# Operand places, piece look-ahead and one job's start in a Fourier-plus-MLP kernel

## The chip, the cores and the metric

The kernel runs on one core of one Trainium2 chip. The metric is device time in microseconds for one execution; lower is better. A core has TensorE (PE, matmuls; PEld its weight loads), VectorE (DVE), ScalarE (ACT), GpSimd (POOL, which here mainly issues DMAs) and SyncE (SP, which only issues DMAs). They run beside each other and wait for each other by semaphores. SBUF is the on-chip memory of 128 partitions, PSUM holds the results of matmuls in eight banks.

## What is computed

x has 2048 rows (tokens) and 640 columns. It is normalized, and three terms are added: x itself, the real part of a two-dimensional Fourier transform, and an MLP that mixes tokens. All is float32.

```python
x = A_x
xn = _layernorm(x, axis=-1)
# A: Fourier mixing
a = einsum("bsd,ed->bse", xn, dft_hid_re)
b = einsum("bsd,ed->bse", xn, dft_hid_im)
A = einsum("ts,bse->bte", dft_seq_re, a) - einsum("ts,bse->bte", dft_seq_im, b)
# B: token MLP, on layernorm(xn) again
u = gelu(einsum("bsd,sf->bdf", _layernorm(xn), w1) + b1)      # F = 1728
B = (einsum("bdf,fs->bds", u, w2) + b2).transpose(0, 2, 1)
return x + A + B
```

## The kernel before

**Pieces.** Every product of two float32 operands is made of three matmuls: each operand is cut into a high part (ACT copies it to float32r, line 131) and a low part (DVE subtracts, line 134); then come high x high, high x low and low x high (`three`, lines 139 to 144). An operand that is used once is a *piece*: `cut_piece` (161) gives its `top` (the ACT copy) and its `bottom` (the DVE subtraction). The pieces lie in three tiles of 5,120 bytes a partition (tags cut0 to cut2), taken in turn. An operand that is used often is cut once and kept.

**Steps and turns.** The work on PE is a list of `steps`, each with the top and the bottom of its piece and its matmuls. `turn_of(i)` (921) writes turn i into the queues: the loads due then, the reads (PSUM copies and adds), the row stages' sums, the top of the piece of step i + AHEAD (AHEAD is 2), the extras (in the column passes the sums of raw pieces), timed work, one or more *jobs* from a list, the bottom of that same piece, more jobs, and last the matmuls of step i. This order is written out by hand; each engine works its queue off in order.

**Stages.** They follow each other on PE:
- *First columns* (`first_columns`, 422): 18 steps, 240 matmuls of 512 columns, for the first block of the sequence transform, while x arrives and is normalized. The order of the first turns is the string START (45); from step 8 on the turns run in the loop at 946. At turn 10 five PSUM copies are due (`reads[10]`, 456, the copies themselves on line 448), at 16 and 18 five more.
- *Column passes* (`columns`, 493), seven of 32 steps and 216 matmuls of 512 columns: the stationary operand is a part of the kept rows (tile n, four slabs of 16,384 bytes), the moving one a piece of the transform's matrix. The first three passes use rows 0 to 1023, in slabs 0 to 3, the last four rows 1024 to 2047, in slabs 4 to 7. In each pass, seven products take the place of eight (Strassen's scheme), so raw pieces are added and subtracted in place (DVE, line 137), two sums at a time, at fixed steps of the pass; the raw pieces come in by DMA from SP, sixteen for each pass, with names B11 to B22 for their quarter. The steps' stationary operand changes slab from step to step: (i, q) uses slab q, or 4 + q in the last four passes.
- *Row stages* (`row_steps`, 697): hid (8 x 7 steps), up0 and up1 (7 x 7 each), down0 and down1 (8 x 7 each), with matmuls of 320 columns. Here the piece is the stationary operand (640, 512 or 384 columns) and the kept tiles shid, sup and sdown, in the same slabs, are the moving one.

**Jobs.** What prepares kept operands is cut into jobs and handed to later turns. The first sums (24 jobs for slabs 0 to 3: `sums_of_rows`, 272) enter the list at turn 9 (867); the rows of slabs 4 to 7 (42 jobs) at turn 18 (875). Up to turn 17 a turn takes two jobs, one ahead of the bottom and one behind it; from 18 on the tables at 56 tell.

**Places.** A tile gets its place in SBUF when its tag is first declared, one behind the other, each rounded up to 32 bytes. In order, with bytes a partition: b1_sb (56), b2_sb (64), slab4 and slab5 (17,920 each), `one` (4), slab7 (17,920), mv, norm and again (128 each), slabs 0 to 3 (17,920 each), the two tiles of raw pieces (16,384 and 17,920), two of 6,144, the three for pieces, v (5,120), slab6 (17,920), and the small working tiles.

Of the kernel before, what the change touches and what calls it, by code (L numbers as in the profile page):

```python
# [8 lines left out]
F32 = mybir.dt.float32  # L9
R32 = mybir.dt.float32r  # L10
# [4 lines left out]
P = 128  # L15
S = 2048
D = 640
F = 1728
NS = S // P
ND = D // P  # L20
# [5 lines left out]
CH = 512  # L26
NC = S // CH
H2 = D // 2
EPS = 1e-5
AHEAD = 2  # L30
LOADS = 4
WARM = 13

BLOCK = 18
# [33 lines left out]
def fnet_plus_mixer(  # L68
# [36 lines left out]

    b1_sb = keep.tile([P, NFB], F32, name="b1_sb")
    b2_sb = keep.tile([P, NS], F32, name="b2_sb")
    out_rows = [out[t * P : (t + 1) * P, :] for t in range(NS)]
    x_rows = [x[t * P : (t + 1) * P, :] for t in range(NS)]

# [7 lines left out]
    y_part = [[dram.tile([P, ND, CH], F32, name=f"y{m}{c}") for c in range(NC)] for m in range(2)]  # L118


    one = keep.tile([P, 1], F32, name="one")
    nc.vector.memset(one, 1.0)
    nc.scalar.activation(one, one, AF.Sqrt)
    idle = keep.tile([P, CH], BF16, name="idle", tag="slab7")
# [31 lines left out]
    loads, sums, reads, extras, timed = (defaultdict(list) for _ in range(5))  # L156
    jobs = []

    cut_turn = [0]

    def cut_piece(source, n):

        held = {}

        def top():
            cut_turn[0] = (cut_turn[0] + 1) % (AHEAD + 1)
            held["piece"] = keep.tile([P, 2, D], R32, name="piece", tag=f"cut{cut_turn[0]}")
# [10 lines left out]
    mv = keep.tile([P, NS, 2], F32, name="mv")  # L178

    norm = keep.tile([P, 2, NS], F32, name="norm")  # L180
    again = keep.tile([P, 2, NS], F32, name="again")

    def moments(k, row):
        st = small.tile([P, 2, 6], F32, name="st")
# [219 lines left out]

    pieces = [keep.tile([P, 2, 4, CH], F32, name=f"pieces{i}", tag=("xa", "xb")[i]) for i in range(2)]
    c_place = [keep.tile([P, 3, CH], F32, name="c", tag=tag) for tag in ("ca", "cb")]
    c_turn = [5]
# [83 lines left out]
    def columns(g, h, c):  # L493

        s0 = len(steps)
        raw = [pieces[(g + m) % 2] for m in range(2)]
        banks, cs = {}, {}

        def load(name, q):
            i, m = int(name[1]) - 1, int(name[2]) - 1  # L500
            nc.sync.dma_start(raw[m][:, i, q, :], dft_seq[m * NC + c, 8 * h + q + 4 * i])

        for name, at in (("B11", (-6, -5, -5, -4)), ("B21", (-3, -3, -2, -2)), ("B12", (-2, -1, 0, 0)), ("B22", (1, 2, 3, 4))):
            for q in range(4):
                loads[s0 + at[q]].append(lambda name=name, q=q: load(name, q))

        def b(name, q, n=1):
            t = raw[int(name[2]) - 1][:, int(name[1]) - 1]
            return t[:, q, :] if n == 1 else t[:, q : q + n, :]

        order = [(1, q) for q in range(4)] + [(i, q) for q in range(4) for i in (2, 8)]
        order += [(i, q) for i in (5, 6) for q in range(4)]
        order += [(3, 0), (3, 1)] + [(7, q) for q in range(4)] + [(3, 2), (3, 3)] + [(4, q) for q in range(4)]
        operand = {1: "B11", 2: "B21", 5: "B11", 6: "B11", 3: "B22", 7: "B12", 8: "B12", 4: "B21"}
        for names, at in (
            (("B11", "B12", "B11"), (6, 8)), (("B11", "B22", "B11"), (13, 15)), (("B12", "B22", "B12"), (17, 18)),
            (("B21", "B21", "B11"), (22, 24)),
        ):  # L520
            for e in range(2):
                extras[s0 + at[e]].append(lambda names=names, e=e: sub(*(b(n, 2 * e, 2) for n in names)))

        bank_of = {1: "z", 6: "z", 7: "z", 4: "z", 5: "y", 3: "y", 2: "w"}
        bank_at = {"z": 2 - 2 * (g % 2), "y": 2 * (g % 2), "w": 5}
        fifth_of = {1: (0, 0), 2: (0, 1), 8: (1, 0), 3: (1, 1)}

        def products(i, q):  # L530
            def run(w):
                a = fixed[h][q]
                if q == 0 and i in (1, 2, 5):
                    for e in range(2):
                        banks[bank_of[i], e] = psum[bank_at[bank_of[i]] + e]
                if i in fifth_of:
                    m, low_rows = fifth_of[i]
                    first = q == 0 and i in (1, 8)
                    if first:
                        banks["f", m] = psum[4 + 3 * m]  # L540
                    three(
                        banks["f", m], (fifth(a, 0, low_rows), fifth(a, 1, low_rows)), w,
                        first, q == 3 and i in (2, 3),
                    )
                if i in bank_of:
                    for e in range(2):
                        at = slot[i] * Q + e * P
                        three(
                            banks[bank_of[i], e], (a[:, 0, at : at + P], a[:, 1, at : at + P]), w,
                            q == 0 and i in (1, 2, 5), q == 3,  # L550
                        )
            return run

        for i, q in order:
            steps.append(cut_piece(lambda i=i, q=q: b(operand[i], q), CH) + (products(i, q),))

        def fresh(name, at, key, e, then=None):
            def run():
                cs[name, e] = c_tile()
                nc.scalar.activation(cs[name, e], banks[key, e], AF.Copy)  # L560
                if then:
                    store_y(h, *then, cs[name, e])
            reads[s0 + at].append(run)

        def more(name, at, key, e, then):
            if g == 2 * NC - 2 and name != "C11":

                return fresh(name, at, key, e, then)

            def run():  # L570
                nc.vector.tensor_add(cs[name, e], banks[key, e], cs[name, e])
                store_y(h, *then, cs[name, e])
            reads[s0 + at].append(run)

        for e in range(2):
            fresh("C11", 4, "z", e)
            more("C11", 11 + e, "w", e, (0, c, e))
            last = g == 2 * NC - 2
            fresh("C22", 16, "y", e, (1, c, 2 + e) if last else None)
            fresh("C12", 20, "z", e, (1, c, e) if last else None)  # L580
            more("C12", 28 + e, "y", e, (1, c, e))
            more("C22", 26 + e, "z", e, (1, c, 2 + e))
# [111 lines left out]
        raw_turn[k] = (raw_turn[k] + 1) % (raws[k].shape[1] - 1)  # L694
        return raws[k][:, raw_turn[k], :n]

    def row_steps(stage, nq, load_piece, at, end, bias=(None, None), base=None, earliest=0, each=None, aside=None):


        s0, n = len(steps), nq * P  # L700
# [2 lines left out]
        def load(*names):  # L703
            for name in names:
                raw[name] = raw_slot(n)
                load_piece(raw[name], int(name[1]) - 1, int(name[2]) - 1)
# [59 lines left out]
            return run  # L766

        for e, names in loads_of.items():
            loads[max(s0 + e, earliest)].append(lambda names=names: load(*names))
        for e, fs in sums_of.items():  # L770
            sums[s0 + e].extend(fs)
        for e, i in enumerate(order):
            steps.append(cut_piece(lambda i=i: raw[operand[i]], n) + (products(i),))
            reads[s0 + e + 1].append(read(i))
# [6 lines left out]
    def hidden(n, t, earliest):  # L781
        ts = (t, t + 4)

        def load_piece(to, i, j):
            c, b = divmod(ts[i], CH // P)
            nc.sync.dma_start(to.rearrange("p (j t) -> p j t", j=ND), y_part[j][c][:, :, b * P : (b + 1) * P])

        return row_steps("hid", ND, load_piece, ("ca", "cb")[n % 2], lambda c: collect(c, ts), earliest=earliest)

    def up(stage, r, at):  # L790
        def load_piece(to, i, j):
# [27 lines left out]
        def aside(i, row, half, b):  # L819
# [4 lines left out]

        s0 = row_steps(
            f"up{stage}", 4, load_piece, at, end, earliest=s_up - 4, aside=aside if stage else None,
        )
        return s0

# [34 lines left out]
        loads[4 + 2 * q].append(lambda q=q: later_load(q))  # L864
    for i, k in enumerate((9, 13, 10, 14, 11, 15)):
        extras[8 + i].append(lambda k=k: later_moments(k))
    timed[9].append(lambda: jobs.extend(
        [j for js in first_sums for j in js[:4]] + [j for q in (2, 3, 0, 1) for j in first_sums[q][4:]]
    ))
    for g in range(2 * NC - 1):  # L870
# [42 lines left out]
    def do_jobs(n, short=False):  # L913

        while n > 0 and jobs and not (short and isinstance(jobs[0], tuple)):
            f = jobs.pop(0)
            n -= 1
            if f:
                (f[0] if isinstance(f, tuple) else f)()

    def turn_of(i, ahead, behind=0, short=False):
        j = i + AHEAD
        for f in loads.pop(i, ()):
            f()
        for f in reads.pop(i, ()):
            f()
        for f in sums.pop(i, ()):
            f()
        if 0 <= j < len(steps):
            steps[j][0]()  # L930
        for f in extras.pop(i, ()):
            f()
        for f in timed.pop(i, ()):
            f()
        do_jobs(ahead, short)
        if 0 <= j < len(steps):
            ready[j] = steps[j][1]()
        do_jobs(behind)
        if 0 <= i < len(steps):
# [3 lines left out]
    with tc.manual_schedule():  # L943
        for word in START.split():
            start[word[0]](*map(int, word[1:].split("-")))
        for i in range(8, len(steps) + 1):
            n_jobs, short = (1, i < BLOCK), False
            if BLOCK <= i < s_hid - 6:
                n_jobs = [(i - BLOCK) % GROUP in at for at in JOBS_AT[i >= s_half]]
            elif i >= s_hid:  # L950
# [4 lines left out]
    assert not (jobs or ready or loads or sums or reads or extras or timed)  # L955


# [38 lines left out]
```

## Time and profile before

| what | us |
|---|---|
| median of 3 runs | 889.89 (889.85 to 891.39) |
| profiled execution, its span | 888.1 |
| PE busy | 880.6 |
| DVE busy | 706.3 |
| ACT busy | 528.8 |
| POOL busy | 123.2 |

The span runs from the first to the last instruction of one profiled execution; what lies around it is in the runs' times and not in the span. A row of a group reads: line, engine, operation, output<-inputs, shape, count, then busy time, mean of one in ns, and the idle time of the engine just before with what ended it. A row of the timeline has start, duration, engine, line and operation, and in brackets the idle time before with its releaser. A row of the stretches has the stretch, its length, and for each engine the busy time and the number of instructions in it, then the granted TensorE clock, the DMA engines' busy share and GB/s. Ends of matmuls are modelled, and a matmul's row overlaps with the next one: what one costs is seen from start to start.

### The profile page before, as it was taken

Reading aid. Unit: us, or ns where it says so; the run is one execution under the profiler, and the core shown is the slowest. Engines: PE = TensorE matmul, PEld = TensorE weight load, DVE = VectorE, ACT = ScalarE, POOL = GpSimd, SP = SyncE. Lnnn points to the kernel's source line nnn. Section 1 sums busy time; section 2 is a strip of 40 time slices with the busy share of each in tenths; the row PEclk is TensorE's granted clock in tenths of the full one; section 3 lists DMA queues with packets and bytes.
Section 4 is the critical chain, followed back from the end, with each engine's and each line's share of the span. In section 5 each row is a group of like instructions: output and inputs, shape, how many; then the busy total and the mean of one; then the engine's idle time right before and its main releaser. Section 6 shows DMA issues by size and latency. Waiting matters only on the chain.

```text
span 888.1 us, 14004 instructions
## 1 busy us (share of the span) xinstructions
PE 880.6 (99%) x4957; PEld 798.4 (90%) x4957; DVE 706.3 (80%) x1183; ACT 528.8 (60%) x956; POOL 123.2 (14%) x166
## 2 busy tenths in 40 slices
PE   9999999999999999999999999999999999999998
PEld 6787878888888878888999999999999999999998
DVE  7877878785888878588787887998678968887776
ACT  6756575754556555457555555675477765655553
POOL 0110100101121111222010101000121211111111
PEclk9999999999999999999999999999999999999999
DMA  7762554619384554958776667454478797757775
GB/s 274 242 235 79 176 215 126 243 59 343 60 218 84 159 121 98 239 74 161 172 151 159 159 136 208 155 165 150 122 178 184 175 255 167 167 130 132 153 174 126
DMA packets 85685, 147.14 MB, mean 166 GB/s; under 512 B 8432, under 2 KB 35568, under 8 KB 85360
## 3 DMA queue, kind: packets, MB, share of 16 engines
q1 hardware_dynamic: 64848, 95.56, 33.0%
q0 software_dynamic: 20624, 50.54, 30.3%
q8 instruction: 39, 0.64, 0.3%
q14 instruction: 30, 0.25, 0.1%
q10 hardware_dynamic: 144, 0.16, 0.1%
HBM read 99.63 MB, written 51.84 MB: 171 GB/s over the span
## 4 chain that ended last, share of the span: by engine, by line
PE 88%; DVE 5%; DMA 3%; ACT 2%; issue 1%; SPq 0%; DVEq 0%
PE psum L143 29%; PE psum L144 29%; PE psum L142 28%; PE psum L440 3%; DMA pieces<-in_dft_seq 2%; DVE piece L134 1%; DMA out<-in_x 1%; ACT piece L131 1%; DMA pieces<-y 1%; DVE n L134 1%; DVE pieces L137 1%; DVE st L186 1%; ACT x L233 1%; ACT n L233 0%; DVE shid L134 0%
## 5 line engine op out<-in xcount | busy, mean ns | idle before, releaser
L134 DVE TENSOR_TENSOR piece<-pieces,piece 128x512 fp32r<-128x512 f32 (+2 forms) x508 | 347.9, 688 | 143.5 <-ACT piece L131 138.9
L131 ACT ACTIVATE piece<-pieces 128x512 fp32r<-128x512 f32 (+2 forms) x508 | 319.3, 629 | 226.6 <-PE psum L144 154.3
L143 PE MATMUL psum<-piece,n 128*128 128x512 f32 x504 | 198.7, 394 | 1.0 <-DVE piece L134 0.9
L142 PE MATMUL psum<-piece,n 128*128 128x512 f32 x504 | 198.0, 393 | 0.1
L144 PE MATMUL psum<-piece,n 128*128 128x512 f32 x504 | 197.6, 392 | 0.0
L144 PE MATMUL psum<-sup,piece 128*128 128x320 f32 x392 | 121.4, 310 | 0.0
L144 PE MATMUL psum<-sdown,piece 128*128 128x320 f32 x392 | 121.1, 309 | 0.0
L142 PE MATMUL psum<-sup,piece 128*128 128x320 f32 x392 | 121.1, 309 | 0.0
L143 PE MATMUL psum<-sup,piece 128*128 128x320 f32 x392 | 121.0, 309 | 0.0
L142 PE MATMUL psum<-sdown,piece 128*128 128x320 f32 x392 | 121.0, 309 | 0.0
L143 PE MATMUL psum<-sdown,piece 128*128 128x320 f32 x392 | 120.9, 309 | 0.0
L143 PEld LDWEIGHTS psum<-piece,n 128*128 128x128 f32 x504 | 94.8, 188 | 25.4 <-DVE piece L134 4.6
L137 DVE TENSOR_TENSOR pieces<-pieces 128x512 f32<-128x512 f32 (+3 forms) x142 | 112.5, 792 | 2.6
L142 PEld LDWEIGHTS psum<-piece,n 128*128 128x128 f32 x504 | 94.7, 188 | 21.7 <-ACT piece L131 0.5
L144 PEld LDWEIGHTS psum<-piece,n 128*128 128x128 f32 x504 | 94.8, 188 | 20.9
L144 PE MATMUL psum<-shid,piece 128*128 128x320 f32 x280 | 86.8, 310 | 0.3 <-DVE piece L134 0.2
L143 PE MATMUL psum<-shid,piece 128*128 128x320 f32 x280 | 86.5, 309 | 0.0
L142 PE MATMUL psum<-shid,piece 128*128 128x320 f32 x280 | 86.5, 309 | 0.0
L761 ACT ACTIVATE pair<-psum 128x320 f32<-128x320 f32 x104 | 45.3, 435 | 58.7 <-PE psum L144 58.2
L144 PEld LDWEIGHTS psum<-sup,piece 128*128 128x128 f32 x392 | 73.6, 188 | 0.3
L144 PEld LDWEIGHTS psum<-sdown,piece 128*128 128x128 f32 x392 | 73.7, 188 | 0.0
L143 PEld LDWEIGHTS psum<-sdown,piece 128*128 128x128 f32 x392 | 73.6, 188 | 0.0
(98 smaller groups left out, 1110.6 us busy)
## 6 DMA issues: line engine op xcount, KB each, us to landing
pieces<-in_dft_seq SPq DMA_DIRECT2D x128, 256.0 KB, 5.1
pieces<-in_w SPq DMA_DIRECT2D x88, 256.0 KB, 3.4
y<-c POOLq DMA_DIRECT2D x84, 256.0 KB, 5.7
out<-pair POOLq DMA_DIRECT2D x38, 320.0 KB, 5.2
pieces<-y SPq DMA_DIRECT2D x32, 320.0 KB, 3.7
pieces<-in_w SPq DMA_DIRECT2D x32, 192.0 KB, 3.4
out<-in_x SPq DMA_DIRECT2D x16, 320.0 KB, 7.0
up<-pair POOLq DMA_DIRECT2D x8, 640.0 KB, 3.2
```

Source lines behind the costliest of these rows:

```text
L131: nc.scalar.activation(hi, src, AF.Copy)
L134: nc.vector.tensor_sub(lo, src, hi.bitcast(F32))
L137: nc.vector.tensor_sub(to, a, b)
L142: nc.tensor.matmul(psum, wh, mh, start=first, stop=False, skip_group_check=True)
L143: nc.tensor.matmul(psum, wh, ml, start=False, stop=False, skip_group_check=True)
L144: nc.tensor.matmul(psum, wl, mh, start=False, stop=last, skip_group_check=True)
L186: nc.vector.bn_stats(st[:, i, :], row[:, i * H2 : (i + 1) * H2])
L233: nc.scalar.activation(row if to is None else to, row, AF.Identity, scale=by[:, 0, k : k + 1], bias=by[:, 1, k : k + 1])
L440: nc.tensor.matmul(banks[m, j], channels(k, j)[rows], w[cols], start=n == 0 and k == begin, stop=n == 2 and k == end, skip_group_check=True,)
L761: nc.scalar.activation(c, b, AF.Copy)
```

## The change

Three edits, made together.

1. The small tiles mv, norm, again and `one` are declared ahead of all others but b1_sb and b2_sb. None changes in size or use.
2. The three tiles for pieces become one tile of 16,384 bytes, declared ahead of the raw pieces and used as a ring: four slots of 4,096 bytes in the column, up and down stages, three of 5,120 bytes in hid, whose pieces are wider. A piece is prepared three turns ahead of its step instead of two, from step 15 to the end of the column passes and from the eighth step of up0 on; hid and the first seven steps of up0 stay two ahead. Loads and sums that feed the pieces issue one turn earlier where the piece does: in the column passes the loads of B11 and the second pair of sums, in the row stages (but hid and up0's first row) all.
3. The jobs of the first sums enter at turn 10 instead of 9, and turn 10 takes two of them ahead of its bottom.

```diff
-AHEAD = 2
...
     b1_sb = keep.tile([P, NFB], F32, name="b1_sb")
     b2_sb = keep.tile([P, NS], F32, name="b2_sb")
+    mv = keep.tile([P, NS, 2], F32, name="mv")
+    norm = keep.tile([P, 2, NS], F32, name="norm")
+    again = keep.tile([P, 2, NS], F32, name="again")
+    one = keep.tile([P, 1], F32, name="one")
...
-    cut_turn = [0]
+    def cut_place(j, n):
+
+        if n > CH:
+            turn, width = (j - s_hid) % 3, 2 * n
+        else:
+            turn, width = (j - s_hid if j < s_hid else j - s_up + 3) % 4, 2 * CH
+        return cut[:, turn * width : turn * width + 2 * n].rearrange("p (a n) -> p a n", a=2)
 
     def cut_piece(source, n):
 
         held = {}
+        j = len(steps)
 
         def top():
-            cut_turn[0] = (cut_turn[0] + 1) % (AHEAD + 1)
-            held["piece"] = keep.tile([P, 2, D], R32, name="piece", tag=f"cut{cut_turn[0]}")
+            held["piece"] = cut_place(j, n)
             high(held["piece"][:, 0, :n], source())
...
+    cut = keep.tile([P, 8 * CH], R32, name="piece")
     pieces = [keep.tile([P, 2, 4, CH], F32, name=f"pieces{i}", tag=("xa", "xb")[i]) for i in range(2)]
...
-        for name, at in (("B11", (-6, -5, -5, -4)), ("B21", (-3, -3, -2, -2)), ("B12", (-2, -1, 0, 0)), ("B22", (1, 2, 3, 4))):
+        for name, at in (("B11", (-7, -6, -6, -5)), ("B21", (-3, -3, -2, -2)), ("B12", (-2, -1, 0, 0)), ("B22", (1, 2, 3, 4))):
...
-            (("B11", "B12", "B11"), (6, 8)), (("B11", "B22", "B11"), (13, 15)), (("B12", "B22", "B12"), (17, 18)),
+            (("B11", "B12", "B11"), (6, 8)), (("B11", "B22", "B11"), (12, 14)), (("B12", "B22", "B12"), (17, 18)),
...
-            loads[max(s0 + e, earliest)].append(lambda names=names: load(*names))
+            loads[max(s0 + e - ahead, earliest)].append(lambda names=names: load(*names))
         for e, fs in sums_of.items():
-            sums[s0 + e].extend(fs)
+            sums[s0 + e - ahead].extend(fs)
...
-    timed[9].append(lambda: jobs.extend(
+    timed[10].append(lambda: jobs.extend(
...
+    prepared = defaultdict(list)
+    for j in range(10, len(steps)):
+        prepared[j - (2 if j < 15 or s_hid <= j < s_up + 7 else 3)].append(j)
+
     def turn_of(i, ahead, behind=0, short=False):
-        j = i + AHEAD
+        js = prepared.pop(i, ())
...
-        if 0 <= j < len(steps):
+        for j in js:
             steps[j][0]()
...
-        if 0 <= j < len(steps):
+        for j in js:
             ready[j] = steps[j][1]()
...
-            n_jobs, short = (1, i < BLOCK), False
+            n_jobs, short = (1 + (i == 10), i < BLOCK), False
```

In `row_steps` the new argument `ahead` is 1, for hid 0, and for up0's first row 0.

More of the change, by code (lines that the diff above doesn't have):

```diff
@@ L118, in fnet_plus_mixer @@
     y_part = [[dram.tile([P, ND, CH], F32, name=f"y{m}{c}") for c in range(NC)] for m in range(2)]
-    one = keep.tile([P, 1], F32, name="one")
     nc.vector.memset(one, 1.0)
@@ L175, in cut_piece @@
         return top, bottom
-    mv = keep.tile([P, NS, 2], F32, name="mv")
-    norm = keep.tile([P, 2, NS], F32, name="norm")
-    again = keep.tile([P, 2, NS], F32, name="again")
     def moments(k, row):
@@ L695, in raw_slot, with row_steps @@
         return raws[k][:, raw_turn[k], :n]
-    def row_steps(stage, nq, load_piece, at, end, bias=(None, None), base=None, earliest=0, each=None, aside=None):
+    def row_steps(
+        stage, nq, load_piece, at, end, bias=(None, None), base=None, earliest=0, each=None, aside=None, ahead=1,
+    ):
         s0, n = len(steps), nq * P
@@ L786, in load_piece @@
             nc.sync.dma_start(to.rearrange("p (j t) -> p j t", j=ND), y_part[j][c][:, :, b * P : (b + 1) * P])
-        return row_steps("hid", ND, load_piece, ("ca", "cb")[n % 2], lambda c: collect(c, ts), earliest=earliest)
+        return row_steps("hid", ND, load_piece, ("ca", "cb")[n % 2], lambda c: collect(c, ts), earliest=earliest, ahead=0)
     def up(stage, r, at):
@@ L826, in up @@
             f"up{stage}", 4, load_piece, at, end, earliest=s_up - 4, aside=aside if stage else None,
+            ahead=int(len(steps) > s_up),
         )
@@ L954, in fnet_plus_mixer @@
             turn_of(i, *n_jobs, short)
-    assert not (jobs or ready or loads or sums or reads or extras or timed)
+    assert not (jobs or prepared or ready or loads or sums or reads or extras or timed)
 def kernel(**inputs):
```

## The prediction

> **What bounds the kernel now.** I read the page first: the busy shares and the chain that ended last.
>
> ```profile
> span 888.1 us, 14004 instructions
> ...
> PE 880.6 (99%) x4957; PEld 798.4 (90%) x4957; DVE 706.3 (80%) x1183; ACT 528.8 (60%) x956; POOL 123.2 (14%) x166
> ...
> PE 88%; DVE 5%; DMA 3%; ACT 2%; issue 1%; SPq 0%; DVEq 0%
> ```
>
> TensorE is 99% busy and 88% of the chain. But ends of matmuls are modelled, so a busy PE can still lose time between starts. I therefore cut the span at the first matmul of each part in the view by stretches, PE alone: length, busy time, matmuls. The count is one too high in each row, since the matmul still running at the cut is counted again. In order: the first columns, the seven column passes, hid, up0, up1, down0, down1.
>
> ```profile
> 6.69:63.45 56.76, 55.62 (x241) 1.00 0.72 251
> 63.45:113.14 49.69, 49.54 (x217) 1.00 0.42 148
> 113.14:163.32 50.18, 49.83 (x217) 1.00 0.53 193
> 163.32:212.84 49.52, 49.52 (x217) 1.00 0.43 153
> 212.84:263.01 50.17, 50.17 (x217) 1.00 0.63 180
> 263.01:313.21 50.20, 50.20 (x217) 1.00 0.59 138
> 313.21:364.62 51.41, 50.77 (x217) 1.00 0.57 129
> 364.62:414.82 50.20, 50.20 (x217) 1.00 0.74 140
> 414.82:539.02 124.20, 123.85 (x841) 1.00 0.71 161
> 539.02:625.59 86.57, 86.57 (x590) 1.00 0.52 162
> 625.59:711.82 86.23, 86.23 (x590) 1.00 0.72 167
> 711.82:810.39 98.57, 98.57 (x674) 1.00 0.73 174
> 810.39:884.48 74.09, 74.08 (x506) 1.00 0.75 151
> ```
>
> The granted clock is 1.00 in every row, so no throttle explains a difference. The best the rows show is 98.57 us for 672 matmuls of 320 columns in down0, 146.7 ns each, and for 512 columns nine starts in 2.04 us, 226.7 ns each (rows below, 277.02 to 279.06). I take these as floors. The first columns need 240 x 0.2267 = 54.41 us and lose 2.35. A pass needs 216 x 0.2267 = 48.97 and the seven lose 0.72, 1.21, 0.55, 1.20, 1.23, 2.44 and 1.23, together 8.58. Hid needs 840 x 0.1467 = 123.20 and loses 1.00; up0 needs 86.24 and loses 0.33; the others lose nothing. So all that an edit of this kind can win is 2.35 + 8.58 + 1.33 = 12.3 us, 1.4%: the instructions on PE stay as they are, and the 6.69 us ahead of the first matmul and the 3.6 us behind the last are not touched.
>
> **The small tiles.** They add and remove no instruction; they move places. The last four passes hold their stationary operand in slabs 4 to 7, the first three in slabs 0 to 3, with the same work. Twenty steps that hold 132 matmuls (from step 12 to the pass's end), first in pass 2, then in pass 5:
>
> ```profile
> 133.37:163.32 29.95, 29.95 (x133) 1.00 0.57 193
> 282.54:313.21 30.67, 30.67 (x133) 1.00 0.66 158
> ```
>
> Neither row has idle time, yet the second is 0.72 us longer: 232.3 against 226.9 ns a matmul. Inside pass 5, two steps of nine matmuls, the first from slab 5 (starts 274.21 to 276.32), the other from slab 6 (277.02 to 279.06), in the timeline of PE:
>
> ```profile
> 274.21 0.40 PE L142 MATMUL psum<-piece,n 128*128 128x512 f32 x1
> ...
> 276.32 0.39 PE L142 MATMUL psum<-piece,n 128*128 128x512 f32 x1
> ...
> 277.02 0.39 PE L142 MATMUL psum<-piece,n 128*128 128x512 f32 x1
> ...
> 279.06 0.39 PE L142 MATMUL psum<-piece,n 128*128 128x512 f32 x1
> ```
>
> 2.11 us against 2.04, in the same pass, with the same helpers running. So it is the slab, not the pass. Counting the declarations (each rounded up to 32 bytes), slabs 0 to 3 and 6, the raw pieces and the cut pieces all begin 160 bytes past a multiple of 512; slabs 4 and 5 begin 256 past one, slab 7 at 288, because b1_sb, b2_sb and `one` lie ahead and mv, norm and again behind. Moved ahead, the small tiles shift slabs 4 and 5 by 416 bytes and slab 7 by 384: all land on 160, and so do the ring (its slots and halves start at multiples of 512 bytes from its begin) and all else. If this remainder is what costs, 4 x 216 = 864 matmuls go from 232.3 to 226.7 ns: **4.9 us** off. The bounds: at best these 4.9; at worst the clean places become slow too (a rival below). I take 4.9, since slab 6, nearest in kind and clean, has that remainder. The row stages gain nothing from it: down0 streams from slabs 4 to 7 and runs at its floor.
>
> The Trainium skill (TensorE: Matmul & The Clock Gate, "Step-by-step: what each phase is for") gives PE two independent SBUF read ports, so that loading the next weights takes nothing from the running matmul. By that a slab's place could not matter, and this edit would be worth 0. The two steps above, 2.11 and 2.04 us, speak against it in this kernel.
>
> **First sums.** At turn 9 the old order puts two jobs on ACT ahead of the five PSUM copies of turn 10 (timeline, ACT, then PE):
>
> ```profile
> 38.27 0.42 ACT L131 ACTIVATE n<-x 128x256 fp32r<-128x256 f32 x1 [2.20 <-DVE x L285]
> 39.67 0.42 ACT L131 ACTIVATE n<-x 128x256 fp32r<-128x256 f32 x1 [0.98 <-DVE x L137]
> 39.99 2.53 ACT L448 ACTIVATE c<-psum 128x512 f32<-128x512 f32 x5
> ```
> ```profile
> 38.64 0.84 PE L440 MATMUL psum<-piece,n 128*128 128x512 f32 x3
> 40.62 1.22 PE L440 MATMUL psum<-piece,n 128*128 128x512 f32 x3 [1.14 <-ACT c L448]
> ```
>
> The two jobs wait for DVE; the copies wait behind them; step 10 starts at 38.64, issues three matmuls and then needs bank 0. Without the wait its fourth matmul starts at 38.64 + 3 x 0.227 = 39.32, not 40.62: 1.3 us, and the two starts behind it are late by 0.37 more in all (the second copy, and an unhidden weight load), so **1.6 us**. With the jobs moved behind, the copies start when step 9 leaves bank 0, five matmuls before its end (about 37.9 with the drain); at 0.5 us each banks 0 and 1 are free at 38.5 and 39.0, ahead of 39.32 and 39.55. What is late next: the jobs, by one slot. Turn 10 takes one more, so 17 instead of 18 are done by turn 18, and the 66 jobs of this list end in the third pass as before, ahead of the first use of slabs 4 to 7. The top of step 12 comes behind the copies, near 40.5, for a step that starts near 45: covered.
>
> **Three ahead in a ring of four.** Per piece there is still one ACT copy and one DVE subtraction; no instruction is added. The wait for the slot stays the same too: with three slots and two ahead, or four and three, the top issued at turn t waits until PE has finished step t-1. What changes is when the piece is needed: a step later. Who waits for pieces now (weight loads' waits, whole run):
>
> ```profile
> PEld psum L143 <- DVE piece L134: 4.6, 11, 0.9
> ...
> PEld psum L144 <- DVE piece L134: 0.9, 2, 0.5
> ...
> PEld psum L142 <- ACT piece L131: 0.5, 1, 0.5
> ```
>
> Fourteen waits, in bursts where jobs and the pass's sums pile on DVE. The costliest, in pass 6 (DVE, then PE):
>
> ```profile
> 325.34 0.68 DVE L134 TENSOR_TENSOR piece<-pieces,piece 128x512 fp32r<-128x512 f32 x1
> 325.94 1.22 DVE L137 TENSOR_TENSOR pieces<-pieces,pieces 128x1024 f32<-128x1024 f32 x1
> 327.07 0.69 DVE L134 TENSOR_TENSOR piece<-pieces,piece 128x512 fp32r<-128x512 f32 x1
> ...
> 329.41 1.22 DVE L137 TENSOR_TENSOR pieces<-pieces,pieces 128x1024 f32<-128x1024 f32 x1
> 330.55 1.28 DVE L134 TENSOR_TENSOR piece<-pieces,piece 128x512 fp32r<-128x512 f32 x2
> ```
> ```profile
> 327.22 0.39 PE L142 MATMUL psum<-piece,n 128*128 128x512 f32 x1
> 327.81 0.50 PE L143 MATMUL psum<-piece,n 128*128 128x512 f32 x1 [0.21 <-DVE piece L134]
> ...
> 330.45 0.40 PE L142 MATMUL psum<-piece,n 128*128 128x512 f32 x1
> 331.29 0.50 PE L143 MATMUL psum<-piece,n 128*128 128x512 f32 x1 [0.44 <-DVE piece L134]
> ```
>
> The low half done at 327.76 is that of the step begun at 327.22; the one begun at 330.55 belongs to the step of 330.45. One step further ahead, each takes the place of the piece before it on DVE: the first is done at 326.02, ahead of the 1.22 us sum, the second at 329.5 (the piece at 328.81). Both are then 0.9 us or more early. The other stalls of the passes are smaller (at most 0.9 us in one burst, pass 2), and a step is 0.68 to 2.04 us long. The passes' losses are 8.58 - 4.9 = 3.7; I leave 0.4, **3.3 us** off. In the rows, up0's 0.33 goes, and about a third of hid's 1.00, because the last column pieces are done a turn earlier while hid itself stays two ahead: **0.6 us**.
>
> What moves with it: the B11 loads and the rows' loads issue one turn earlier on SP, past no load that they depend on; SP waits for a free place, not for a turn, and the places come free a turn earlier since their last readers (ACT and DVE pieces) do too. The second sums move from turns 13 and 15 to 12 and 14, so that they stand two turns behind the pieces that they overwrite, as now. The POOL stores keep their place. If a load were late the cover is gone and ACT waits; the B21 loads keep four turns, at least 6 us. Turn 12 and the turn at up0's step 4 take two pieces, and one turn before hid takes none: 1.3 us of ACT and DVE work in turns with room. Hid's wider slots overlap two column slots each, but only ones that step t-1 has left.
>
> **The sum**, against the profiled execution: 888.1 - 4.9 - 1.6 - 3.3 - 0.6 = 877.7 us of span. The median of the runs, 889.89, lies 1.8 above that span; with it **879.5 us**.
>
> **The rivals.** (1) It is not the remainder that makes slabs 4, 5 and 7 slow but where they lie: all three are below byte 70,500, slab 6 and the others above, and that stays so. It is also the case in which the edit doesn't do what it is there for. Then 4.9 come back: 884.4. The Trainium skill's rule on the read ports, above, gives the same. Against it: nothing in the rows ties time to low bytes, but nothing excludes it. (2) The stalls stay, because in the bursts DVE has no time to spare whatever the order: 3.3 + 0.6 come back, 883.4. For it: DVE runs without a gap from 324 to 332. Against it: the stalls end as soon as single pieces land, and none recurs for 80 us. (3) **Slower:** the ring leaves byte 189,088 for 142,496, and its halves lie 2,048 apart instead of 2,560. If the slow kind is a clash between the two operands' places, the ring, an operand of every matmul, can carry it to those now clean: 648 + 240 column and 3,192 row matmuls at 5.6 ns are 22.9 us, less 5.5 won elsewhere: about 907. It ends above today's time by more than 1.8 us from 1.8 ns on each of these 4,080. Against it: the remainder by 512 stays 160, and the rows run at one floor with moving operands at several remainders.
>
> **Chances.** The forecast 0.62, its own range 878.2 to 881.0; rival 1 0.18; rival 2 0.10; both at once 0.04, which is 888.3, within 0.2% (1.8 us, about what a measurement of this kernel can tell from no change); rival 3 0.06. So faster 0.90, same 0.04, slower 0.06. The range takes in the forecast and rivals 1 and 2: 878.0 to 885.0.
>
> **What would show it.** In the stretches of the changed kernel, the last four passes near 49.0 us each as the first three, and steps of slabs 4 to 7 alike at 2.04: the places. If they stay at 50.2, rival 1. The five L448 copies on ACT ahead of any L131 into n, and no idle PE between 38 and 42: the first sums. Weight loads' waits for pieces near nothing in the passes, one of about 0.5 us left in hid: the ring. First three passes or rows above their floors without idle time: rival 3. The forecast is wrong if the four passes stay above 49.5.

## The result and the profile after

The median of 4 runs is **882.18 us** (881.5 to 882.7), that of the kernel before, on the same chip, 889.87 (889.75 to 891.39). The ratio is 0.9911, its interval 0.9897 to 0.9925: 0.9% faster. The time is 2.7 us above the forecast: outside the forecast's own range (878.2 to 881.0), and inside the wide one (878.0 to 885.0) that takes in rivals 1 and 2. The page of the changed kernel, its span, busy shares and chain of waits:

```profile
span 880.5 us, 13991 instructions
...
PE 873.3 (99%) x4957; PEld 798.4 (91%) x4957; DVE 704.2 (80%) x1183; ACT 525.0 (60%) x956; POOL 123.5 (14%) x166
...
PE 97%; DMA 1%; DVE 1%; ACT 0%; issue 0%; SPq 0%; DVEq 0%; ACTq 0%
```

The busy shares say nothing (PE was at 99% before, too); the chain does: PE has gone from 88 to 97% of it, so less of the end is set by waits. Where the 7.6 us of span came from, the stretches tell, cut as before at the first matmul of each part (first columns, first and last of the seven passes, which are all 48.96, then hid, up0, up1, down0, down1):

```profile
6.76:61.82 55.06, 55.06 (x241) 1.00 0.78 274
61.82:110.78 48.96, 48.96 (x218) 1.00 0.41 145
...
355.58:404.54 48.96, 48.96 (x218) 1.00 0.73 135
404.54:528.01 123.47, 123.46 (x841) 1.00 0.69 162
528.01:616.32 88.31, 86.88 (x590) 1.00 0.50 158
616.32:702.56 86.24, 86.24 (x591) 1.00 0.74 172
702.56:801.12 98.56, 98.56 (x675) 1.00 0.70 170
801.12:876.83 75.71, 75.67 (x506) 1.00 0.72 148
```

The granted clock is 1.00 in every row. Against before: first columns 56.76 to 55.06, -1.70; passes 351.37 in all to 342.72, -8.65; hid -0.73; **up0 86.57 to 88.31, +1.74; down1 74.09 to 75.71, +1.62**. Together -7.7. So the passes stand at their floor to the last matmul, and two row stages that the prediction expected at their floor have got slower.

The first sums behave as written down. ACT, then PE, in the timeline:

```profile
37.99 2.56 ACT L452 ACTIVATE c<-psum 128x512 f32<-128x512 f32 x5 [2.50 <-PE psum L444]
...
40.91 0.45 ACT L133 ACTIVATE n<-x 128x256 fp32r<-128x256 f32 x1
```
```profile
35.75 6.51 PE L444 MATMUL psum<-piece,n 128*128 128x512 f32 x28
```

The five copies wait for PE alone and come ahead of the jobs, and PE issues 28 matmuls in one row, with no gap.

**Where down1 loses.** Seven of the eight rows of down1, all but the last, have a late matmul at the same place. The second of the seven, on DVE in the changed kernel:

```profile
816.55 0.55 DVE L717 TENSOR_TENSOR pieces<-pieces 128x384 f32<-128x384 f32 x1
817.13 0.56 DVE L139 TENSOR_TENSOR pieces<-pieces 128x384 f32<-128x384 f32 x1
817.61 0.55 DVE L136 TENSOR_TENSOR piece<-pieces,piece 128x384 fp32r<-128x384 f32 x1
818.07 0.48 DVE L761 TENSOR_TENSOR pair<-psum,pair 128x320 f32<-128x320 f32 x1
```

The same place in the kernel before:

```profile
826.43 0.49 DVE L755 TENSOR_TENSOR pair<-psum,pair 128x320 f32<-128x320 f32 x1 [0.16 <-PE psum L144]
826.84 0.55 DVE L711 TENSOR_TENSOR pieces<-pieces 128x384 f32<-128x384 f32 x1
827.42 0.56 DVE L137 TENSOR_TENSOR pieces<-pieces 128x384 f32<-128x384 f32 x1
```

And PE in the changed kernel:

```profile
818.25 0.31 PE L145 MATMUL psum<-sdown,piece 128*128 128x320 f32 x1
818.40 0.31 PE L146 MATMUL psum<-sdown,piece 128*128 128x320 f32 x1
818.70 0.38 PE L144 MATMUL psum<-sdown,piece 128*128 128x320 f32 x1
818.92 0.31 PE L145 MATMUL psum<-sdown,piece 128*128 128x320 f32 x1
```

Before, the read of product 7's PSUM bank (L755) ran first, as soon as PE had left the bank, and the two sums of the next row (L711 and L137) behind it. After, the sums (L717 and L139) are one turn earlier, so they stand in the queue ahead of that read (L761 at 818.07), which ends at 818.55. Product 4 goes on in the same bank and may start only then: the starts are 0.30 and 0.22 us apart, not 0.147 each, 0.23 lost. Six of the places lose 0.23 and the first 0.27, which is 1.65 in all, against 1.62 by the stretches.

**Where up0 loses.** First what the tile of raw pieces shows between 528 and 536 (its load and that load's time to landing), then DVE, then PE:

```profile
L798 SPq DMA_DIRECT2D pieces<-in_w x1: 328/328/328, 529.9 to 529.9; - x1
...
DMA to landing us min/median/max: 4.8/4.8/4.8
```
```profile
534.81 0.69 DVE L139 TENSOR_TENSOR pieces<-pieces 128x512 f32<-128x512 f32 x1 [3.16 <-DMA pieces<-in_w]
...
538.60 1.28 DVE L136 TENSOR_TENSOR piece<-pieces,piece 128x512 fp32r<-128x512 f32 x2
539.80 0.48 DVE L761 TENSOR_TENSOR pair<-psum,pair 128x320 f32<-128x320 f32 x1
```
```profile
535.20 0.31 PE L145 MATMUL psum<-sup,piece 128*128 128x320 f32 x1
536.16 0.41 PE L146 MATMUL psum<-sup,piece 128*128 128x320 f32 x1 [0.66 <-DVE piece L136]
...
539.34 0.31 PE L146 MATMUL psum<-sup,piece 128*128 128x320 f32 x1
540.43 0.38 PE L144 MATMUL psum<-sup,piece 128*128 128x320 f32 x1 [0.78 <-DVE pair L761]
```

The raw pieces of the row stages use seven places in turn. In up0's first row, the difference A12 - A11 is formed at the row's third turn (the row's sums are not shifted). The second row's A12 goes to the place of that A11, and its load, now one turn earlier, is issued in the same turn, where loads come ahead of sums. So DVE stands still for 3.16 us until a load has landed that has nothing to do with its row. In the kernel before, the same difference ran first, and the load was issued right behind it (DVE, then SP's queue, whose row begins with that load):

```profile
542.70 0.69 DVE L137 TENSOR_TENSOR pieces<-pieces 128x512 f32<-128x512 f32 x1
```
```profile
543.46 14.57 SPq L792 DMA_DIRECT2D pieces<-in_w  x5
```

This is more than a delay: **the changed kernel takes the difference with the second row's A12 in the place of A11**, so product 3 of up0's first row is wrong, and with it the values of 128 hidden features in columns 320 to 639. It is a fault of the change. Of the kernels below that start from the changed one, row sums back, one load later and split sums put the load behind the difference again; the others keep the fault.

In the changed kernel, PE loses 0.82 at 536.16, and once more 0.94 at 540.43, where DVE, late by then, has its sums and the two pieces of the turn that takes two (538.60) ahead of the PSUM read at 539.80.

### The profile page after: what moved, and what is told of

Same layout as the page of the kernel before. It is cut to its first block, busy times and chain, and to the rows that moved or that the text cites. A ratio compares the mean times of both kernels' runs of the same rounds, so it can differ in the third digit from the quotient of the medians.

```text
span 880.5 us, 13991 instructions
## 1 busy us (share of the span) xinstructions
PE 873.3 (99%) x4957; PEld 798.4 (91%) x4957; DVE 704.2 (80%) x1183; ACT 525.0 (60%) x956; POOL 123.5 (14%) x166
## 4 chain that ended last, share of the span: by engine, by line
PE 97%; DMA 1%; DVE 1%; ACT 0%; issue 0%; SPq 0%; DVEq 0%; ACTq 0%
PE psum L144 31%; PE psum L146 30%; PE psum L145 30%; PE psum L444 6%; DMA pieces<-in_w 1%; DMA pieces<-in_dft_seq 0%; DVE piece L136 0%; ACT piece L133 0%; DVE pieces L139 0%; DVE pair L761 0%; DVE pieces L717 0%; ACT n L236 0%; DVE pair L763 0%; SPq L468 0%; DVE r L205 0%
## 5 line engine op out<-in xcount | busy, mean ns | idle before, releaser
L144 PE MATMUL psum<-piece,n 128*128 128x512 f32 x504 | 196.1, 389 | 0.0
L145 PE MATMUL psum<-piece,n 128*128 128x512 f32 x504 | 196.1, 389 | 0.0
L146 PE MATMUL psum<-piece,n 128*128 128x512 f32 x504 | 196.1, 389 | 0.0
L139 DVE TENSOR_TENSOR pieces<-pieces 128x512 f32<-128x512 f32 (+3 forms) x142 | 112.6, 793 | 6.0 <-DMA pieces<-in_w 3.2
L144 PEld LDWEIGHTS psum<-sdown,piece 128*128 128x128 f32 x392 | 73.6, 188 | 1.6 <-issue 1.6
L144 PEld LDWEIGHTS psum<-sup,piece 128*128 128x128 f32 x392 | 73.6, 188 | 1.2 <-issue 1.0
L146 PEld LDWEIGHTS psum<-sup,piece 128*128 128x128 f32 x392 | 73.6, 188 | 0.9 <-DVE piece L136 0.9
```

The source lines that it names most:

```text
L139: nc.vector.tensor_sub(to, a, b)
L144: nc.tensor.matmul(psum, wh, mh, start=first, stop=False, skip_group_check=True)
L145: nc.tensor.matmul(psum, wh, ml, start=False, stop=False, skip_group_check=True)
L146: nc.tensor.matmul(psum, wl, mh, start=False, stop=last, skip_group_check=True)
```

## The experiments

The theory after the first look: the places are worth what was forecast, and the rows lose by order in DVE's queue, plus one load. The rivals: the rows lose by the ring's new places or by three-ahead itself; and the places act by where they lie, not by a remainder. Single runs vary by some 2 us (the kernel before from 889.75 to 891.74), so the parts of the profiled executions decide. The parts in us, cut in the same way:

| kernel | first columns | passes 1-3 (mean) | passes 4-7 (mean) | hid | up0 | up1 | down0 | down1 | span |
|---|---|---|---|---|---|---|---|---|---|
| before | 56.76 | 49.80 | 50.50 | 124.20 | 86.57 | 86.23 | 98.57 | 74.09 | 888.1 |
| after | 55.06 | 48.96 | 48.96 | 123.47 | 88.31 | 86.24 | 98.56 | 75.71 | 880.5 |
| places only | 56.77 | 49.81 | 49.42 | 123.91 | 86.59 | 86.24 | 98.56 | 74.08 | 883.5 |
| old places | 55.07 | 48.96 | 50.19 | 123.19 | 88.29 | 86.24 | 98.56 | 75.72 | 885.0 |
| jobs at turn 9 | 56.78 | 48.96 | 48.96 | 124.48 | 88.26 | 86.24 | 98.56 | 75.70 | 883.1 |
| row sums back | 55.07 | 48.96 | 48.96 | 123.20 | 89.52 | 89.54 | 100.68 | 74.98 | 886.0 |
| one load later | 55.10 | 48.96 | 48.96 | 123.94 | 86.71 | 86.24 | 98.56 | 75.72 | 879.3 |
| split sums | 55.06 | 48.96 | 48.96 | 123.19 | 86.24 | 86.24 | 98.56 | 74.09 | 876.7 |
| all at 256 | 55.08 | 48.96 | 48.96 | 123.20 | 88.77 | 86.24 | 98.56 | 75.71 | 880.9 |
| ring at 256 | 56.37 | 50.40 | 50.30 | 123.01 | 88.11 | 86.24 | 98.56 | 75.75 | 890.7 |
| slab offsets | 55.11 | 48.96 | 49.63 | 123.20 | 87.90 | 86.24 | 98.56 | 75.71 | 882.5 |

**Places only.** The kernel before with edit 1 alone.

```diff
     b2_sb = keep.tile([P, NS], F32, name="b2_sb")
+    mv = keep.tile([P, NS, 2], F32, name="mv")
+    norm = keep.tile([P, 2, NS], F32, name="norm")
+    again = keep.tile([P, 2, NS], F32, name="again")
+    one = keep.tile([P, 1], F32, name="one")
...
-    one = keep.tile([P, 1], F32, name="one")
...
-    mv = keep.tile([P, NS, 2], F32, name="mv")
-    norm = keep.tile([P, 2, NS], F32, name="norm")
-    again = keep.tile([P, 2, NS], F32, name="again")
```

> The kernel before with the small tiles declared first and nothing else. Theory (a slab's bytes modulo 512 against the ring's decide): the passes over slabs 4 to 7 fall from 50.20 us to 48.97 each where no piece is late, pass 6 to about 50.2 with its stalls, and the span by 4.9 us to about 883.2; the first three passes, the first columns and the rows stay. Rival (the gain of those passes in the changed kernel came with the ring's own move or the look-ahead): they stay near 50.2, the span near 888.

One run of 886.81 us, beside a median of 890.37 for the kernel before; span 883.5, 4.6 less. Its stretch of pass 5:

```profile
261.89:310.99 49.10, 49.10 (x218) 1.00 0.60 141
```

Passes 4, 5 and 7 fall by 1.1 to 1.2 us without a change of one instruction. Pass 6 falls by 0.9, since it keeps its burst of waits for pieces. Up0 and down1 stay at 86.59 and 74.08: what they lose after is not from the places of the small tiles.

**Old places.** The changed kernel with the four small tiles where they were.

```diff
-    mv = keep.tile([P, NS, 2], F32, name="mv")
-    norm = keep.tile([P, 2, NS], F32, name="norm")
-    again = keep.tile([P, 2, NS], F32, name="again")
-    one = keep.tile([P, 1], F32, name="one")
...
+    one = keep.tile([P, 1], F32, name="one")
...
+    mv = keep.tile([P, NS, 2], F32, name="mv")
+    norm = keep.tile([P, 2, NS], F32, name="norm")
+    again = keep.tile([P, 2, NS], F32, name="again")
```

> The changed kernel with the small tiles back where they were: slabs 4 and 5 begin 256 bytes past a multiple of 512, slab 7 at 288, the ring and the others at 160. Theory: the last four passes are at 50.2 us again without idle time, steps of slab 6 at 2.04 to 2.05 us for nine matmuls and the others at 2.10; the first three stay at 48.96; span 880.5 + 4.9 = 885.4. Rival (the ring's new place cured them): 48.96 in all seven, span 880.5.

One run of 886.99 us, span 885.0. Pass 5:

```profile
258.75:308.95 50.20, 50.20 (x217) 1.00 0.57 135
```

Each of the four passes is back at 50.2 with no idle time, 4 x 1.23 = 4.9 us, and the first three are untouched. The rows lose as after. (The span rises by 4.5 only: hid was 0.3 shorter in this run.) From the other side, in the run above, the four passes give 4 x 1.08 = 4.3 us, since late pieces still take some of it there.

**Jobs at turn 9.** Edit 3 alone undone.

```diff
-    timed[10].append(lambda: jobs.extend(
+    timed[9].append(lambda: jobs.extend(
...
-            n_jobs, short = (1 + (i == 10), i < BLOCK), False
+            n_jobs, short = (1, i < BLOCK), False
```

> The changed kernel with the jobs of the first sums entering at turn 9 again and one job ahead at turn 10. Theory (two jobs that wait for DVE stand ahead of the five PSUM copies on ACT): PE stands still near 39 again, the first columns rise from 55.06 by 1.6 to 1.7 us to 56.7, all passes stay at 48.96, span about 882.1. Rival (the ring of four lets the copies through in time either way): the first columns stay near 55.1, span 880.5.

One run of 885.19 us; first columns 56.78, 1.72 more than after, and the wait is back where it was (ACT, then PE):

```profile
39.73 0.42 ACT L133 ACTIVATE n<-x 128x256 fp32r<-128x256 f32 x1 [0.98 <-DVE x L139]
40.05 2.53 ACT L452 ACTIVATE c<-psum 128x512 f32<-128x512 f32 x5
```
```profile
40.68 3.50 PE L444 MATMUL psum<-piece,n 128*128 128x512 f32 x13 [1.16 <-ACT c L452]
```

So edit 3 is worth 1.7 us, and the ring does not replace it. Hid came out at 124.48 here, 1.0 more than after with the same code in hid; over all runs it lies between 123.01 and 124.48. No edit explains that spread, and what sets it was not settled.

**Row sums back.** The sums of the row stages, and their later loads, at the turns of before; pieces still three ahead.

```diff
-            loads[max(s0 + e - ahead, earliest)].append(lambda names=names: load(*names))
+            loads[max(s0 + e - (ahead if e == -6 else 0), earliest)].append(lambda names=names: load(*names))
...
-            sums[s0 + e - ahead].extend(fs)
+            sums[s0 + e].extend(fs)
```

> The changed kernel, but in the row stages the sums of raw pieces and the load of A12 issue at their old turns; the pieces stay three ahead, the other three loads a turn earlier. Theory (up0's and down1's new losses come from sums that stand ahead of a PSUM read on DVE and, once, behind a load): down1 falls from 75.71 to 74.1 us, up0 from 88.31 to 86.3 to 87.3 (two pieces still share one turn), span 877.0 to 878.0, median 878.8 to 879.8. Rival (the look-ahead itself overloads DVE and ACT in the short steps of down1): down1 stays near 75.7 and the span near 880.

888.45 us, median of 10 runs; ratio to before 0.9979 (0.9969 to 0.9989). As a remedy it failed: down1 gains 0.7 of its 1.6, while up0, up1 and down0 get 1.2, 3.3 and 2.1 us longer than after. ACT, DVE and PE in down0:

```profile
787.94 0.63 ACT L133 ACTIVATE piece<-pieces 128x512 fp32r<-128x512 f32 x1 [2.10 <-DVE pieces L139]
...
789.10 0.51 ACT L765 ACTIVATE pair<-psum,b_sb 128x320 f32<-128x320 f32 x1
```
```profile
787.16 0.69 DVE L139 TENSOR_TENSOR pieces<-pieces 128x512 f32<-128x512 f32 x1
```
```profile
789.66 0.42 PE L144 MATMUL psum<-sdown,piece 128*128 128x320 f32 x1 [0.93 <-ACT pair L765]
```

Now a top that is made three turns ahead needs a sum of its own turn. ACT stands for 2.10 us until DVE has done it (787.16), and the PSUM read behind it on ACT (789.10) is what PE waits for. So the sums cannot all stay where they were: some of them must move with the pieces, and the queue decides which. Early sums block a read on DVE; late ones block a read on ACT.

**One load later.** The changed kernel, with the A12 load of up0's second row one turn later, behind the difference that reads its place.

```diff
-            loads[max(s0 + e - ahead, earliest)].append(lambda names=names: load(*names))
+            late = stage == "up0" and s0 == s_up + 7 and e == -4
+            loads[max(s0 + e - (0 if late else ahead), earliest)].append(lambda names=names: load(*names))
```

> The changed kernel with one load a turn later, that of A12 of up0's second row, so that it follows the subtraction of the first row that reads the same place. Theory (that subtraction waits for the load's landing): the stall of 0.8 us in up0's fifth step goes, up0 falls by about 0.9 us from 88.31 to 87.4 or less, down1 stays at 75.7, span about 879.5. Rival (DVE is full there whatever the load): up0 stays at 88.3.

One run of 881.63 us; span 879.3. DVE's timeline, then the stretch of up0:

```profile
531.33 0.69 DVE L136 TENSOR_TENSOR piece<-pieces,piece 128x512 fp32r<-128x512 f32 x1 [1.07 <-ACT piece L133]
532.05 0.69 DVE L139 TENSOR_TENSOR pieces<-pieces 128x512 f32<-128x512 f32 x1
```
```profile
528.38:615.09 86.71, 86.62 (x590) 1.00 0.50 161
```

The difference comes right behind the piece, without a wait, and up0 loses 0.47 in place of 2.07: the one load made both of its stalls, all but this rest, which goes with the next edit. The difference also gets the right A11 again, and the kernel is faster for it, so the gain over the kernel before does not come from the fault. Down1 stays at 75.72, as it should.

**Split sums.** As the last, and of the two sums that moved together only the one that the next top needs stays early; A11 - A21, needed three turns later, goes one turn on, behind the PSUM read.

```diff
-            -2: (first_sum, lambda: sub(raw["A21"], raw["A11"], raw["A21"])),
-            -1: (lambda: sub(raw["A11"], raw["s"], raw["A11"]),),
+            -2: (first_sum,),
+            -1: (lambda: sub(raw["A21"], raw["A11"], raw["A21"]), lambda: sub(raw["A11"], raw["s"], raw["A11"])),
```

> The changed kernel with the late load mended as in the run with one load later, and of the row stages' early sums only the first (A21 + A22) at its new turn; the difference for A21 goes one turn on, beside the one for A11, behind the turn's PSUM read on DVE. Theory (a PSUM read that stands behind both sums on DVE holds the bank that PE wants): down1 falls from 75.7 to 74.1 us, up0 to 86.3 to 86.8, no ACT top waits for a sum of its own turn, span 877.0 to 877.7, median 878.9 to 879.8. Rival (ACT tops block behind the later sums, as in the run with the sums at their old turns): up0 and up1 lose 1 us or more each, span above 879.

**878.62 us**, median of 4 runs (878.5 to 878.72); ratio to before 0.9867 (0.985 to 0.9885), below the interval of the changed kernel. Stretches of up0 and down1, then PE's waits in the whole run (line, what it waited for, us in total, times, longest):

```profile
527.62:613.86 86.24, 86.24 (x590) 1.00 0.51 162
...
798.66:872.75 74.09, 74.08 (x506) 1.00 0.75 151
```
```profile
PE psum L130 <- DVE idle L127: 1.2, 1, 1.2
PE psum L444 <- ACT n L236: 1.1, 1, 1.1
```

Every pass and every row stage stands at its floor, with nothing but two waits at the very start left. One DVE subtraction of 0.56 us, moved behind one read, is worth 1.62 us in down1: that settles the cause there.

**Three kernels on the places.** The changed kernel with spare bytes declared between the tiles, so that all instructions stay and only places move. First all slabs, raw pieces and the ring at 256 past a multiple of 512, in place of 160; then only the ring, the raw pieces and slab 6 (declared behind them) at 256 and the other slabs at 160; then the ring and slabs 0 to 3 and 6 at 416, slab 4 at 160, slab 5 at 352, slab 7 at 384 (256, 64 and 32 below the ring's remainder); there a small working tile shares another's place to make room.

```diff
     one = keep.tile([P, 1], F32, name="one")
+    pad = keep.tile([P, 24], F32, name="pad")
```

> The changed kernel with 96 unused bytes behind the small tiles: all slabs, the ring and the raw pieces begin 256 bytes past a multiple of 512. Theory A (what counts is the distance between the slab's place and the ring's): all seven passes stay at 48.96 us, span 880.5. Theory B (what counts is a place's own remainder, and 160 is a good one): all seven at about 50.2, span about 889.

```diff
+    pad = keep.tile([P, 24], F32, name="pad")
     cut = keep.tile([P, 8 * CH], R32, name="piece")
```

> The changed kernel with 96 unused bytes ahead of the ring: ring, raw pieces and slab 6 at 256 modulo 512, slabs 0 to 5 and 7 at 160. Theory A (distance): the first three passes rise to 50.2 us or more, in the last four only the steps of slab 6 are clean (2.04 us for nine matmuls), span about 888 to 890. Theory B (own remainder of the stationary operand): the first three passes stay at 48.96, of the last four only slab 6's steps are slow, span about 882.

```diff
-    x_slab = [
-        keep.tile([P, 7, D], F32, name="x0", tag="slab4"), keep.tile([P, 1, D], F32, name="x1", tag="slab5"),
-    ]
+    x_slab = [keep.tile([P, 7, D], F32, name="x0", tag="slab4")]
+    pad0 = keep.tile([P, 48], F32, name="pad0")
+    x_slab.append(keep.tile([P, 1, D], F32, name="x1", tag="slab5"))
+    pad1 = keep.tile([P, 8], F32, name="pad1")
...
+    pad2 = keep.tile([P, 8], F32, name="pad2")
...
-            var = small.tile([P, NS], F32, name="var2")
+            var = small.tile([P, NS], F32, name="var2", tag="r")
```

> The changed kernel with unused bytes between the slabs: modulo 512 the ring, slabs 0 to 3 and 6 at 416, slab 4 at 160, slab 5 at 352, slab 7 at 384, so 256, 64 and 32 below the ring; the small tile var2 shares another's place. Theory A (distance): the first three passes and slab 6 clean at 226.7 ns a matmul; which of the three distances is slow says what the distance is counted by: slab 4 clean means 256 or a divisor of it, slab 7 or 5 clean a divisor of 32 or 64. Theory B (own remainder): slab 4, at 160, clean and all others slow, 416 among them.

One run each: 882.87, 892.74 and 884.52 us, beside 890.56 for the kernel before. A pass of the first, then a pass of the second:

```profile
208.59:257.55 48.96, 48.96 (x217) 1.00 0.64 185
```
```profile
63.06:113.46 50.40, 50.40 (x217) 1.00 0.40 139
```

At 256 everywhere nothing is slow, although 256 was the remainder of the slow slabs 4 and 5 before. With the ring and what is declared behind it moved by 96, slabs 0 to 3, which no edit had ever made slow, are: 50.40 / 216 = 233.3 ns a matmul in place of 226.7. So it isn't a place's own remainder; what tells the cases apart is the **distance of the two operands modulo 512**. The raw pieces share the ring's remainder in every run, so a slab might also clash with what DVE and ACT read and write while PE works. The starts in passes 1 to 3 of the second kernel speak against that: they are 232.7 ns apart where DVE is idle and ACT busy (71 matmuls), 233.2 where DVE is busy and ACT idle (189) and 232.7 where both are busy (212). The third kernel, PE, steps of nine matmuls from slab 4, 5 and 7 (starts of the first and of the one behind the last):

```profile
316.25 0.39 PE L146 MATMUL psum<-piece,n 128*128 128x512 f32 x1
...
318.29 0.39 PE L146 MATMUL psum<-piece,n 128*128 128x512 f32 x1
...
318.97 0.39 PE L146 MATMUL psum<-piece,n 128*128 128x512 f32 x1
...
321.03 0.39 PE L146 MATMUL psum<-piece,n 128*128 128x512 f32 x1
...
324.45 0.40 PE L146 MATMUL psum<-piece,n 128*128 128x512 f32 x1
...
326.55 0.40 PE L146 MATMUL psum<-piece,n 128*128 128x512 f32 x1
```

In these steps 256 below costs nothing (2.04 us), 64 a little (2.06), 32 the full price (2.10), like 96 and 128 before. But the clean slabs are not clean in every step. In passes that hold slow slabs too, some of their steps of nine take up to 2.09 us: with slab 6 of the second kernel, which has the ring's own remainder, two of three in each pass (the third takes 2.05); with slab 4 of the third kernel one or two of three (2.07), with its slab 6 two (2.05 and 2.08); with slab 6 of the kernel before two (2.05 to 2.07). In passes without a slow slab and without a wait all steps take 2.04. That a slow step carries over to the one behind it would fit, but was not tested; what in the chip makes the distance count stays open.

## Why the prediction came out as it did

- **The places, 4.9 us forecast:** 4.9 measured in the passes when edit 1 is taken out of the changed kernel, 4.3 when it alone is put into the kernel before. Rival 1, that their low location counts, fell with the changed kernel itself: slabs 4, 5 and 7 still lie low and run at 48.96 a pass. The remainder was the right sign to read but not the whole rule; it is a matter of two places, and the edit puts both at 160. The prediction took a place's own remainder as the cause and left the clash of two places to a rival, so this term was right in part by luck: it held because the ring came out at 160 as well. The Trainium skill's two independent read ports (TensorE: Matmul & The Clock Gate, "Step-by-step: what each phase is for") would have given 0; 233.3 ns against 226.7, with nothing changed but a place, disagree.
- **First sums, 1.6:** 1.70, by the mechanism told.
- **Column stalls, 3.3:** 3.7 (2.5 in passes 1 to 3, 1.2 in pass 6 above its 50.20). The 0.4 that were held back went too. Rival 2, that DVE is full whatever the order, fell: it is as busy as before, and no wait is left in the passes. The runs with the places only (49.81 in passes 1 to 3) and with the jobs at turn 9 (48.96) leave edit 2 as the cause; whether its third turn, its earlier sums or its earlier loads did it was not run apart.
- **The rows, 0.6 off: this step failed; they gave 2.6 us back.** Hid -0.73, up0 +1.74, down1 +1.62. The prediction said that what moves goes "past no load that they depend on", that work comes into "turns with room", and costed it at nothing. It counted busy time and dependences between loads, and left out two things. The sums shifted with the pieces were not followed past the PSUM reads in DVE's queue, and the load of up0's second row was not held against the unshifted sum of the first row, which still reads the place: the prediction named "ACT and DVE pieces" as the last readers, and here the last one is a sum. Splitting the sums and holding that load back brings up0 and down1 to 86.24 and 74.09, so these two are all of it. Hid's gain is no proof of the ring, by its spread above.
- **The sum:** 877.7 of span forecast, 880.5 measured. The 2.8 us are the rows (3.2 the wrong way) less the stalls (0.4) and first sums (0.1), with 0.1 more at the ends. That the time lies inside the wide range is owed to rivals 1 and 2, which had widened it and did not come. The split-sums kernel, in which the rows are as the prediction took them, has 876.7.
- **Rival 3, the clash carried to clean operands,** did not come, but it was a real risk: the ring at a distance of 96 costs 10.2 us of span against after, and the one run of that kernel, 892.74, lies above the kernel before (889.75 to 891.26). Its price of 22.9 was too high, since the row matmuls do not take part: up1, down0 and down1 are the same in all three kernels on the places.

## What to carry to other kernels

When work is prepared earlier, write down each engine's queue around the new place, and look above all for reads that free a PSUM bank: move only what the next step needs, and leave the rest behind the read. Where loads move past a reader of their destination, the order between two rows changes even if each row alone is in order, and the reader then waits for the new data and takes it for the old. And where a stretch of PE has no idle time but differs between equal passes, compare the places of its two operands before looking for waits.

## What the runs showed of the hardware

The distance between stationary and moving operand (modulo 512) has a price. With 512 columns a matmul takes 226.7 ns at a distance of 0 in every pass where all slabs have it, 233 to 234 on average at 32, 96 and 128, and 229 at 64; at 256, 226.7 in the clean steps of the one slab that had it, beside slow slabs. Steps of clean slabs in passes with slow ones take up to 2.09 us per nine in place of 2.04. The matmuls of 320 columns keep their floor in all of these runs (down0 98.56 throughout, but for the waits of the kernel with the row sums back).

And in up0 and down1 of the changed kernel a stop costs more than its length: the next start behind it, too, comes late by 0.07 to 0.11 us (540.43 to 540.65, 0.22 in place of 0.147). Of the 0.23 that a late matmul of down1 costs, too short for the list of waits, 0.07 is of this kind.
